# A fused attention and channel-mix kernel: when the loads of batch 1 are issued, and which engine does three small steps of block 0

## The chip, the cores and the metric

The kernel runs on one core of a Trainium2 chip. The metric is the time of one execution on the device in microseconds (us). A profile's span is about 1.8 us shorter than the time of the same execution, so spans are compared with spans and times with times.

## The reference

Cross-covariance attention over four batches of 6208 rows and 256 columns, then a channel mix:

```python
qn = q / (norm(q, axis=1) + 1e-6); kn = k / (norm(k, axis=1) + 1e-6)
a = softmax(kn.transpose(0, 2, 1) @ qn / tau, -1)        # 256 x 256 for each batch
x = v @ a
x_prev = x shifted down by one row, zero first
xk = mu_k * x + (1 - mu_k) * x_prev                      # xr the same with mu_r
k = maximum(xk @ w_k, 0)                                 # 256 -> 1024
out = sigmoid(xr @ w_r) * ((k * k) @ w_v)
```

## The kernel before

The softmax weights of batch 0 need all q and k of batch 0, so the first 36 us read them and sum their products. A serial stretch follows: norms, roots, inverses, scaling, transposes, exp, shares. Then a long loop works on 512-row blocks of x and takes in the products of q and k of batches 1 to 3 between its own. The parts that matter here, with cuts marked by `...`:

```python
v_load(1)                                       # GpSimd queue, in this order
nc.gpsimd.dma_start(w_k_sb, ...)
next_load()                                     # q, k of batch 1, first group
nc.gpsimd.dma_start(w_r_sb, ...)
v_load(2)
nc.gpsimd.dma_start(w_v_sb, ...)
v_load(3)
next_load()
difference, product = x_first()
root(1); root(0)
...
turn_half, take_half = v_first()
invert_first(0)                                 # VectorE, 128x2
evac_first()                                    # VectorE: scale s by 1/|q|
turn_half(0)                                    # TensorE: first half of v of block 0
turn()                                          # TensorE: transpose s
turn_half(1)
keep_warm(2)
go = v_transpose_pe(1, nc.scalar.copy)          # v of block 1
invert_first(1)
take_half(0, nc.vector.tensor_copy)             # first half of v out of PSUM
difference(0)
exp()                                           # ScalarE
go()
weigh_first(0); weigh_first(1)                  # VectorE: shares, a_sb = e * share
take_half(1, nc.vector.tensor_copy)
difference(1)
for a in range(2): ...                          # x and xk of block 0

# in the loop (i = block - 1, j = 0..7)
if i == -1 and j < 3:
    for fh, a in (((0, 0), (1, 0), (0, 1)), ((1, 1),), ())[j]:
        up_first(fh, a)                         # 128 hidden rows, half a block
    if j == 2:
        up(0, 2)
...
if 0 < i + 2 < NBLK and j in (0, 2) and full:
    x_half(i + 2, int(j > 0))                   # 128 columns of x of block i + 2

def up(i, fh): ...
    if fh % 4 == 0 and (i or fh):               # output of the relus: four rows of hidden tiles a buffer
        st[i, "kr", fh // 4] = p2.tile([P, 4, M], BF16, name="kr", tag="kr", bufs=2)
    kr = st[i, "kr", fh // 4][:, fh % 4, :m]
    nc.scalar.activation(kr, kT_ps[:, :m], AF.Relu, scale=0.5 ** 0.5)
```

`square` then reads a `kr` buffer on VectorE (four hidden tiles in one instruction, later two), and frees it. Two such buffers exist.

## Time and profile before

| | before |
|---|---|
| time, median of the first 3 runs | 505.31 us (504.74 to 506.22) |
| span of the profile | 503.1 us |
| TensorE busy | 96% of the span |
| VectorE, ScalarE busy | 85% each |
| serial stretch from the roots to the second x of block 1 | 35.8 to 44.8 us |

How to read it: TensorE is the chain that ended last from 44.8 us on, without a gap. As long as its products stay the same, a kernel of that kind gets shorter only by what moves the start of that unbroken run and opens no gap in it.

### The profile page before, as it was taken

How to read it: one execution, taken by the hardware profiler on the slowest of the kernel's cores; microseconds unless marked ns; L12 is line 12 of the kernel's file. 1: busy time of each engine (PE TensorE's matmuls, PEld its weight loads, DVE VectorE, ACT ScalarE, POOL GpSimd, SP SyncE). 2: the span in 40 equal slices, each digit the busy share in tenths (PEclk: the TensorE clock that was granted, in tenths of full speed). 3: DMA queues.
4: the chain of work that ended last, by engine and by line, in shares of the span. 5: the costliest groups of instructions: out<-in, count | busy, mean ns of one | idle time of the engine just before them, and what ended most of it. 6: DMA issues, size and time to landing. Idle time of an engine off the chain costs nothing.

```text
span 503.1 us, 9303 instructions
## 1 busy us (share of the span) xinstructions
PE 482.3 (96%) x3437; PEld 331.2 (66%) x3437; DVE 429.7 (85%) x787; ACT 428.2 (85%) x871; POOL 96.9 (19%) x143
## 2 busy tenths in 40 slices
PE   2789999999999999999999999999999999999996
PEld 1355677677666766666776666676666666666675
DVE  2788899999988998999889899899888787878784
ACT  4788999899999989888999898988888888788884
POOL 0044322222233132122123323100031010000000
PEclk9999999999999999999999999999999999999999
DMA  8999999999799999997799999982295658344123
GB/s 328 418 314 197 196 185 176 209 210 195 149 187 179 202 166 177 146 203 116 142 191 146 197 171 183 168 150 65 66 207 103 152 86 156 77 105 86 56 71 106
DMA packets 131558, 83.46 MB, mean 166 GB/s; under 512 B 50548, under 2 KB 125624, under 8 KB 130488
## 3 DMA queue, kind: packets, MB, share of 16 engines
q0 software_dynamic: 55840, 33.01, 49.8%
q1 hardware_dynamic: 75352, 49.59, 39.9%
q8 instruction: 27, 0.44, 0.4%
q10 hardware_dynamic: 320, 0.26, 0.2%
q14 instruction: 19, 0.16, 0.1%
HBM read 78.71 MB, written 25.43 MB: 207 GB/s over the span
## 4 chain that ended last, share of the span: by engine, by line
PE 92%; DMA 4%; ACT 2%; DVE 1%; issue 0%; SPq 0%; ACTq 0%; DVEq 0%
PE vr_ps L603 33%; PE kT_ps L571 33%; PE vr_ps L599 8%; PE xT_ps L465 8%; PE s_ps L293 6%; DMA f<-in_k_dram 4%; ACT k L160 1%; PE s_ps L199 1%; ACT qk L155 1%; PE st_ps L353 0%; PE y_ps L643 0%; PE kT_ps L511 0%; PE bank L217 0%; PE vT_ps L425 0%; DVE xk L498 0%
## 5 line engine op out<-in xcount | busy, mean ns | idle before, releaser
L576 ACT ACTIVATE kr<-kT_ps 128x512 bf16<-128x512 f32 (+1 forms) x390 | 234.9, 604 | 33.4 <-PE kT_ps L571 29.7
L603 PE MATMUL vr_ps<-w_v_sb,kk 128*128 128x256 bf16 x1536 | 230.3, 273 | 0.0
L571 PE MATMUL kT_ps<-xk,w_k_sb 128*128 128x512 bf16 (+1 forms) x780 | 229.8, 377 | 0.0
L603 PEld LDWEIGHTS <-kk 128*128 128x128 bf16 x1536 | 150.3, 98 | 57.3
L584 DVE TENSOR_TENSOR kk<-kr 128x2048 bf16<-128x2048 bf16 (+1 forms) x148 | 125.7, 850 | 0.2 <-ACT kr L576 0.2
L613 DVE SCALAR_TENSOR_TENSOR res<-res,vr_ps 128x256 f32<-128x256 f32 x192 | 80.0, 416 | 50.1 <-ACT res L612 50.1
L571 PEld LDWEIGHTS <-w_k_sb 128*128 128x128 bf16 x780 | 75.5, 98 | 27.5 <-issue 0.6
L612 ACT ACTIVATE res<-vr_ps 128x256 f32<-128x256 f32 x192 | 76.7, 399 | 1.3 <-PE vr_ps L603 1.3
L599 PE MATMUL vr_ps<-w_r_sb,xr 128*128 128x256 bf16 x384 | 73.3, 273 | 0.0
L467 ACT CAST xT<-xT_ps 128x512 bf16<-128x512 f32 x94 | 55.9, 595 | 20.0 <-PE xT_ps L465 19.7
L556 DVE SCALAR_TENSOR_TENSOR xr<-delta,mu_t,xT 128x512 bf16<-128x512 bf16 x94 | 70.0, 746 | 0.0
L556 DVE SCALAR_TENSOR_TENSOR xk<-delta,mu_t,xT 128x512 bf16<-128x512 bf16 x94 | 70.0, 745 | 0.0
L599 PEld LDWEIGHTS <-xr 128*128 128x128 bf16 x384 | 37.6, 98 | 44.5 <-issue 0.2
L133 POOL DMA_DIRECT2D qk<-in_q_dram x39 | 26.0, 668 | 169.3 <-ACT kr L576 147.7
L465 PE MATMUL xT_ps<-vT,a_sb 128*128 128x512 bf16 x188 | 55.9, 379 | 0.0
L293 PE MATMUL s_ps<-qk 128*128 128x256 bf16 (+1 forms) x294 | 55.8, 273 | 0.0
L254 ACT ACTIVATE sq<-qk 128x1024 bf16<-128x1024 bf16 x48 | 51.0, 1063 | 0.0
L408 POOL DMA_DIRECT2D v_bf<-in_v_dram x47 | 35.6, 759 | 67.3 <-DMA vT<-v_bf 48.7
L199 PE MATMUL s_ps<-qk 128*128 128x384 bf16 (+2 forms) x98 | 20.2, 357 | 14.8 <-ACT qk L155 14.8
L546 DVE TENSOR_TENSOR delta<-xT 128x1024 bf16<-128x1024 bf16 x47 | 32.2, 686 | 1.1 <-ACT xT L467 1.1
L293 PEld LDWEIGHTS <-qk 128*128 128x128 bf16 (+1 forms) x294 | 28.5, 98 | 5.6 <-issue 0.8
L133 POOL DMA_DIRECT2D qk<-in_k_dram x39 | 25.9, 665 | 3.4 <-DMA w_k_sb<-in_moe_w_k_dram 2.0
(113 smaller groups left out, 252.7 us busy)
## 6 DMA issues: line engine op xcount, KB each, us to landing
out_dram<-res SPq DMA_DIRECT2D x47, 512.0 KB, 4.7
v_bf<-in_v_dram POOLq DMA_DIRECT2D x47, 256.0 KB, 7.3
qk<-in_q_dram POOLq DMA_DIRECT2D x36, 256.0 KB, 6.1
qk<-in_k_dram POOLq DMA_DIRECT2D x36, 256.0 KB, 7.3
f<-in_q_dram SPq DMA_DIRECT2D x4, 1024.0 KB, 13.3
f<-in_k_dram SPq DMA_DIRECT2D x4, 1024.0 KB, 11.0
f<-in_q_dram SPq DMA_DIRECT2D x3, 512.0 KB, 7.6
f<-in_k_dram SPq DMA_DIRECT2D x3, 512.0 KB, 6.2
```

What stands on the lines that cost most here:

```text
L133: nc.gpsimd.dma_start(rows_at(qk, b, g, i)[:rows, :n], qk_src(t, b, g))
L293: nc.tensor.matmul(s_ps[:, ih, :], rows_at(qk, b, g, 0)[:rows, s, ih * P:(ih + 1) * P], rows_at(qk, b, g, 1)[:rows, s, :], start=t0 and ih ...
L465: nc.tensor.matmul(xT_ps, a_sb[:, b, ih, dh * P:(dh + 1) * P], vT[:, :, ih, :], start=ih == 0, stop=ih == 1)
L467: nc.scalar.copy(xT[:, dh, 1:], xT_ps)
L556: nc.vector.scalar_tensor_tensor(o[:, dh], st[i, "d"][:, dh], mu[:, dh:dh + 1], st[i, "x"][:, dh, :M], op0=OP.mult, op1=OP.add)
L571: nc.tensor.matmul(kT_ps[:, :m], w_k_sb[:, dh, fh * P:(fh + 1) * P], xk[:, dh, :m], start=dh == 0, stop=dh == 1)
L576: nc.scalar.activation(kr, kT_ps[:, :m], AF.Relu, scale=0.5 ** 0.5)
L584: nc.vector.tensor_tensor(st[i, "kk"][:, fh // 4 * 4 + lo:fh + 1, :m], kr, kr, op=OP.mult)
L599: nc.tensor.matmul(vr_ps[:, D:], xr[:, dh, s * P:(s + 1) * P], w_r_sb[:, dh, :], start=dh == 0, stop=dh == 1)
L603: nc.tensor.matmul(vr_ps[:, :D], kk[:, fh, s * P:(s + 1) * P], w_v_sb[:, fh, :], start=fh == 0, stop=fh == 7)
L612: nc.scalar.activation(res[:, s], vr_ps[:, D:], AF.Tanh, scale=0.5)
L613: nc.vector.scalar_tensor_tensor(res[:, s], res[:, s], 1.0, vr_ps[:, :D], op0=OP.add, op1=OP.mult)
```

## The change

Its intent: keep GpSimd from writing DMA descriptors while VectorE does the inverses; relieve VectorE of half of v and ScalarE of two relus; fill a hole of TensorE with x of block 1. The diff, cut to its core:

```diff
+    held = const.tile([P, 1], F32, name="held")
 ...
     v_load(1)
     nc.gpsimd.dma_start(w_k_sb, ...)
-    next_load(); w_r_sb; v_load(2); w_v_sb; v_load(3); next_load()
 ...
     go = v_transpose_pe(1, nc.scalar.copy)
+    take_half(0, nc.scalar.copy)
     invert_first(1)
-    take_half(0, nc.vector.tensor_copy)
+    nc.gpsimd.tensor_copy(held, chain_done())     # reads the inverse of the norm of k
+    next_load(); w_r_sb; v_load(2); w_v_sb; v_load(3); next_load()
     difference(0)
 ...
-        nc.scalar.activation(kr, kT_ps[:, :m], AF.Relu, scale=0.5 ** 0.5)
+        if i == 0 and fh in (2, 3):
+            nc.vector.tensor_scalar(kr, kT_ps, 0.0, 0.5 ** 0.5, op0=OP.max, op1=OP.mult)
+        else:
+            nc.scalar.activation(kr, kT_ps[:, :m], AF.Relu, scale=0.5 ** 0.5)
 ...
-                for fh, a in (((0, 0), (1, 0), (0, 1)), ((1, 1),), ())[j]:
+                for fh, a in (((0, 0), (1, 0)), ((1, 1),), ())[j]:
                     up_first(fh, a)
+                if j == 0:
+                    x_half(1, 0)
+                    up_first(0, 1)
 ...
-                if j in (0, 2) and full:
+                if j in (0, 2) and full and (i, j) != (-1, 0):
```

(The loads are shortened to their names.) As in the prediction, part 1 is the hold, part 2 the ScalarE copy, part 3 the earlier x, part 4 the relus on VectorE.

More of the change, by code (lines that the diff above doesn't have):

```diff
@@ L376, in softmax_pieces @@
         if b == 0:
-            return diagonals, root, invert_first, evac_first, turn, exp, weigh_first
+            return lambda: rk[:, 0:1], diagonals, root, invert_first, evac_first, turn, exp, weigh_first
         return [evac, None, norms, roots, pow2, None, invert, None, None, turn, lambda: exp([0]), lambda: exp([1]),
@@ L664, in keep_warm @@
             nc.tensor.matmul(junk_ps, ones, fill, start=True, stop=True)
-    diagonals, root, invert_first, evac_first, turn, exp, weigh_first = softmax_pieces(0)
+    chain_done, diagonals, root, invert_first, evac_first, turn, exp, weigh_first = softmax_pieces(0)
     pending = []
@@ L731 @@
     nc.gpsimd.dma_start(w_k_sb, moe_w_k.rearrange("(ko ki) f -> ki ko f", ki=P))
-    next_load()
-    nc.gpsimd.dma_start(w_r_sb, moe_w_r.rearrange("(ko ki) d -> ki ko d", ki=P))
-    v_load(2)
-    nc.gpsimd.dma_start(w_v_sb, moe_w_v.rearrange("(fo fi) d -> fi fo d", fi=P))
-    v_load(3)
-    next_load()
     difference, product = x_first()
@@ L749 @@
     go = v_transpose_pe(1, nc.scalar.copy)
+    take_half(0, nc.scalar.copy)
     invert_first(1)
-    take_half(0, nc.vector.tensor_copy)
+    nc.gpsimd.tensor_copy(held, chain_done())
+    next_load()
+    nc.gpsimd.dma_start(w_r_sb, moe_w_r.rearrange("(ko ki) d -> ki ko d", ki=P))
+    v_load(2)
+    nc.gpsimd.dma_start(w_v_sb, moe_w_v.rearrange("(fo fi) d -> fi fo d", fi=P))
+    v_load(3)
+    next_load()
     difference(0)
```

## The prediction

> **What bounds the kernel now.** I read the page first, then the chain of waits in order of time, then the timelines of the engines around the hand-over from the first phase (covariance of batch 0) to the long loop, then the time to landing of the transfers. From the page:
>
> ```profile
> PE 482.3 (96%) x3437; PEld 331.2 (66%) x3437; DVE 429.7 (85%) x787; ACT 428.2 (85%) x871; POOL 96.9 (19%) x143
> PE 92%; DMA 4%; ACT 2%; DVE 1%; issue 0%; SPq 0%; ACTq 0%; DVEq 0%
> ```
>
> TensorE is 92% of the chain that ended last. The rest is the first 44 us: input loads, then a serial softmax for batch 0. The chain of waits between 35 and 45 us (start, length, what):
>
> ```profile
> 35.76 0.27 ACT rn L322 x2
> 36.03 0.02 issue
> 36.05 0.48 DVE rn L325
> ...
> 38.20 0.24 PE vT_ps L444 x4
> 38.44 0.03 issue
> 38.47 0.44 DVE vT L447
> 38.93 0.43 DVE delta L479
> 39.35 0.08 DVE sm L373
> ...
> 42.53 0.28 PE kT_ps L511
> 42.84 0.39 ACT kr L513
> 43.23 0.04 issue
> 43.27 0.40 PE kT_ps L511 x2
> 43.67 0.43 PE xT_ps L465 x2
> ```
>
> See three things. A VectorE instruction on 128x2 numbers takes 0.47 us at 36.05. A copy of half of v plus a difference (38.47 to 39.35) stand on VectorE ahead of the reciprocal that the softmax weights wait for. And at 43.23 TensorE, with nothing ahead of it, waits for a relu. From 44.8 us on the chain is TensorE without a gap, so whatever moves that point moves the end; nothing else in this change can. A gain of 2% would be 10.1 us, more than the whole 35.76 to 44.78 stretch (9.0 us), so the sign of a fraction of a microsecond is the real question.
>
> The timeline of the same stretch gives durations (start, length, instruction):
>
> ```profile
> 35.70 0.16 DVE L227 TENSOR_SCALAR less<-mu_t 128x4 f32<-128x4 f32 x1
> 36.05 0.47 DVE L325 TENSOR_SCALAR rn<-rn 128x2 f32<-128x2 f32 x1 [0.19 <-ACT rn L322]
> 37.63 0.34 DVE L325 TENSOR_SCALAR rn<-rn 128x2 f32<-128x2 f32 x1
> 38.47 0.43 DVE L447 COPY vT<-vT_ps 128x512 bf16<-128x512 bf16 x1 [0.30 <-PE vT_ps L444]
> 46.03 0.69 DVE L546 TENSOR_TENSOR delta<-xT 128x1024 bf16<-128x1024 bf16 x1 [1.11 <-ACT xT L467]
> ```
>
> The copy at 38.47 waits for the second group of v transposes, though it reads only what the first group wrote. In the built program its wait is indeed on the last of the second group.
>
> **What the Trainium skill says.** "SBUF — State Buffer", section "Who interferes with whom": VectorE in a two-port mode and GpSimd share a pair of ports under an exclusive lock, and the one that comes second blocks for the whole instruction. The trace agrees in kind: the two L325 took 0.474 and 0.342 us while POOL was writing descriptors, and a like-sized one 0.164 us; casts L157 of 512 columns took 0.61 and 0.67 us under POOL issues, against 0.69 us for 1024 columns. "DMA: Bandwidth & Descriptors", section "Queues, rings and completion order": a DMA engine consumes a ring's descriptors in order. The trace agrees: the GpSimd queue lands in the order of issue. From issue times plus times to landing w_k comes at 34.0 + 7.0 = 41.0 us, w_r at 35.8 + 8.5 = 44.3, w_v at 37.0 + 11.2 = 48.2. "VectorE: DVE Perf Modes", section "Why PSUM operands drop a tier": an fp32 operand in PSUM holds VectorE to its slowest mode. The trace's 128x256 forms from PSUM take 0.416 us (L498, L613).
>
> **The change part by part.**
>
> 1. *Batch 1 loads held.* A one-column GpSimd copy now waits for the second inverse (its wait count is the one that exp has), so POOL writes no descriptors between about 34.7 and 37.7 us. Removed from the path: the excess of the first L325, 0.474 − 0.164 = 0.31 us. Does holding starve the DMA? No: w_k alone keeps the engines busy to 41.0, and the held issues restart near 38, each 0.55 to 0.95 us to issue against 1.25 us or more to move. So I expect the same landings: w_v at 48.2 against a first use at 50.2, v of block 2 at 45.6 (36.5 issue plus its landing) against 47.4. Because the queue is in order, w_k is not faster either. But POOL will now write descriptors from 38 to 43 without the pause that it had (39.3 to 41.3), and that covers the two a_sb scalings (L374, 0.353 us each, SBUF to SBUF). Each may be held up to 0.3 us; as the middle I take 0.15 (one like instruction of 128x256, L341, ranges from 0.336 to 0.494). Cost: 2 × 0.15 = 0.30 us.
>
> 2. *Half of v on ScalarE.* In the built program the ScalarE copy carries the same wait as before, the end of the second v transposes, and it stands ahead of exp on the in-order engine. Exp used to wait only for the transposes of s. With part 1 the second v transposes end at 38.43 − 0.31 = 38.12. A 512-column ScalarE copy takes 0.59 us (as L467) with the next one starting 0.48 to 0.50 later: exp starts at 38.64 (before: 38.27). From exp's start to its accumulator is 0.56 us (38.27 to 38.83 before), so the first reciprocal starts at 39.24 and the first weighing at 39.43, before 39.46. VectorE's relief is thus paid back by the delay of exp: parts 1 and 2 together give 0.03 us by the weights, and with the POOL conflict of part 1 they cost 0.27 us. Everything to the first xk (41.60) hangs behind that.
>
> 3. *x of block 1 earlier.* Before, TensorE had issued the first two up products by 42.86 and then waited to 43.27. The x products of block 1 (2 × 0.22 us of issue) now fill that hole. Later x waits for ScalarE to empty the first half: before 44.73, now about 44.28 as the relu of the third product no longer stands ahead of that copy. TensorE gains 0.43 to 0.45 us at 44.78.
>
> 4. *Two relus on VectorE.* They cost 128x512 from PSUM in fp32: 0.416 us for 256 columns plus 256 more at 1.04 ns makes 0.68 us each, 1.36 us. VectorE idled 1.11 us before delta (46.03), so delta moves to about 46.5 (one relu must also wait for its product), delta 0.69, two xk 1.42: xk of block 1 is done at 48.65 instead of 48.18. TensorE, 0.43 early, wants the second xk at 48.47, so it waits about 0.21. Left of part 3: 0.22 us. The squares end at about 50.95, before the need of 51.1; VectorE's next idle time (1.52 us ahead of the first res, 53.35) takes up the rest. ScalarE loses 2 × 0.57 us, which is no bound here since TensorE has no gap.
>
> Sum: −0.31 + 0.28 (exp behind the copy, net of VectorE's relief) + 0.30 (POOL against the weights) − 0.43 (x earlier) + 0.21 (xk late) = +0.05 us; without the POOL conflict −0.25 us. I lean somewhat to the gain, since the conflict is a matter of chance and ScalarE gets 1.1 us of slack just where it is busiest: −0.2 us, 505.1.
>
> **The rivals.**
>
> - *A clean gain of about 1 us.* For it: if relief of ScalarE lets TensorE run earlier, or the conflict with POOL slowed more than the one L325. Against: no gap of TensorE after 44.8 names ScalarE. It would give 504.3.
> - *A loss by the copy ahead of exp.* If the ScalarE copy with its strided output takes longer than 0.59 us, and both a_sb are blocked the full 0.3 us, parts 1 and 2 cost up to 0.7 us and only 0.2 comes back: 505.8.
> - *Loads late.* If the held loads leave the queue empty, w_v slips. For it: they start 3 us later. Against: the transfers are in order and the queue is full to 41.0. If it slipped by the full 3 us, w_v would land at 51.2, TensorE would lose 1 us and the first units of batch 1 might wait too: about 506.3.
> - *Nothing moves the end.* If the loop's later waits (transposes, POOL's refills) set its pace, 505.3. The chain shows TensorE alone there, so I give it little.
>
> **Range and chances.** The three runs of before span 504.74 to 506.22, 1.5 us, as much as any rival is worth. I put the range at 503.9 to 506.2: from the clean gain less 0.4 of spread, to the late loads without spread. None comes near 10 us, so within 2% is almost certain.
>
> **What would show it.** In the changed kernel's profile: the first L326 (the former L325) near 0.17 us and POOL silent until about 37.7; exp's first start near 38.6 behind the ScalarE copy; the two weighings 0.35 us if free of POOL, 0.5 or more if not, with the second ending near 40.2 or 40.5; x of block 1 directly after the first two up products with no gap of 0.25 us; VectorE relus of 0.68 us; a wait of about 0.2 us for xk near 48.5; w_v landing near 48.2. I am wrong if exp does not move, if w_v lands after 50 us, or if TensorE shows new gaps after 50 us.

## More of the kernel before

All runs but one took 503.8 to 506.6 us; that one took 575.22 us, at a mean granted TensorE clock of 0.854, and is called slow, the others fast. Comparisons of times are of fast runs.

In every trace of this study whose state is fast, the time from the first product for x of block 4 to that of block 20 is 156.8 us, and that from x of block 3 to the end is 444.1 to 444.2 us. Whatever a variant gains or loses is therefore settled within the first 60 us. I use the start of x of block 3 (58.9 us in the kernel before) as the ruler for it.

## The result, and the profile after

The changed kernel took 505.44 us (median of 4, 505.16 to 505.67) against 505.02 (504.70 to 506.22) of the kernel before in the same rounds. The ratio is 1.0004, with a 95% interval of 0.9986 to 1.0022: the same. A repeat of five rounds gave 505.14 against 504.82, ratio 1.0003 (0.9990 to 1.0017).

The page of the changed kernel, engine totals and chain shares:

```profile
PE 481.8 (96%) x3437; PEld 330.9 (66%) x3437; DVE 429.7 (85%) x788; ACT 428.1 (85%) x870; POOL 97.2 (19%) x144
PE 89%; DVE 3%; DMA 3%; ACT 2%; issue 1%; SPq 1%; ACTq 0%; DVEq 0%
```

TensorE's share of the chain fell from 92% to 89% while its busy time stayed, and VectorE rose from 1% to 3%. So something other than TensorE now carries part of the early stretch. The chain of waits of the changed kernel (start, length, what):

```profile
38.13 0.24 PE vT_ps L445 x4
38.37 0.02 issue
38.39 0.59 ACT vT L448
38.98 0.47 ACT e_sb L362 x2
...
44.72 0.69 DVE kr L578
45.41 0.78 DVE xr L499 x2
46.20 0.60 DVE kr L578
46.79 0.61 DVE delta L547
...
47.43 1.42 DVE xk L557 x2
48.84 1.15 DVE kk L588
...
50.09 0.30 ACT kr L580
```

Two things are new. The ScalarE copy of v (38.39) stands in the chain ahead of exp. And from 44.7 to 50.0 us the chain is VectorE, where before it was TensorE: the two relus, xr, delta, xk and the square. Then it goes on over ScalarE and VectorE, and TensorE has it again from 57.8 us. The timeline of the changed kernel (start, length, instruction, idle time before it and what ended that):

```profile
36.28 0.17 DVE L326 TENSOR_SCALAR rn<-rn 128x2 f32<-128x2 f32 x1 [0.20 <-ACT rn L323]
37.98 0.17 POOL L750 COPY held<-rn 128x1 f32<-128x1 f32 x1 [2.89 <-DVE rn L327]
47.55 0.62 PE L426 MATMUL vT_ps<-ident,v_bf 128*128 128x128 bf16 x8 [0.28 <-DMA v_bf<-in_v_dram]
50.09 0.60 ACT L580 ACTIVATE kr<-kT_ps 128x512 bf16<-128x512 f32 x1 [0.37 <-DVE kk L588]
```

The inverse is quick and GpSimd is silent until 37.98, as intended. TensorE waits for v of block 2, which it did not before. ScalarE waits for a square on VectorE, because the relu's output needs the buffer which that square frees.

From 44.52 us (second x of block 1, 0.26 us sooner than before) to x of block 3 at 59.52 us took 15.0 us. Before it was 14.13 us (44.78 to 58.91). So the lead was gained and then more than lost, all between 44 and 60 us. The starts of TensorE's products show where: beyond their usual spacing (0.22 us after a product of 512 columns, 0.11 after 256) they fall behind by 0.44 us at v of block 2 (47.55) and by 0.43 us at 55.9 and 57.8.

### The profile page after: what moved, and what is told of

It is laid out like the page before. It is cut to its first block, busy times and chain, and to the rows that moved or that the text cites. A ratio compares the mean times of both kernels' runs of the same rounds, so it can differ in the third digit from the quotient of the medians.

```text
span 503.7 us, 9299 instructions
## 1 busy us (share of the span) xinstructions
PE 481.8 (96%) x3437; PEld 330.9 (66%) x3437; DVE 429.7 (85%) x788; ACT 428.1 (85%) x870; POOL 97.2 (19%) x144
## 4 chain that ended last, share of the span: by engine, by line
PE 89%; DVE 3%; DMA 3%; ACT 2%; issue 1%; SPq 1%; ACTq 0%; DVEq 0%
PE vr_ps L607 33%; PE kT_ps L572 32%; PE vr_ps L603 8%; PE xT_ps L466 8%; PE s_ps L294 6%; DMA f<-in_k_dram 3%; ACT k L161 1%; PE s_ps L200 1%; SPq L126 1%; DVE kk L588 0%; PE st_ps L354 0%; DVE xk L557 0%; ACT qk L156 0%; PE y_ps L647 0%; DVE k L168 0%
## 5 line engine op out<-in xcount | busy, mean ns | idle before, releaser
L603 PEld LDWEIGHTS <-xr 128*128 128x128 bf16 x384 | 37.6, 98 | 44.7 <-issue 0.4
L466 PE MATMUL xT_ps<-vT,a_sb 128*128 128x512 bf16 x188 | 55.9, 379 | 0.0
```

What stands on the lines that cost most here:

```text
L466: nc.tensor.matmul(xT_ps, a_sb[:, b, ih, dh * P:(dh + 1) * P], vT[:, :, ih, :], start=ih == 0, stop=ih == 1)
L603: nc.tensor.matmul(vr_ps[:, D:], xr[:, dh, s * P:(s + 1) * P], w_r_sb[:, dh, :], start=dh == 0, stop=dh == 1)
```

## The experiments

Twelve runs were made, five rounds each (six for combined), two of them repeats; all were correct. The column "against before" is the mean time of a kernel's fast runs less that of the kernel before in the same rounds. With standard deviations of 0.1 to 0.4 us in five runs (1.0 in the six of combined), such a difference is uncertain by about 0.2 us, and all the 95% intervals of the ratios but one hold 1. The ratios differ from those of these means by up to 0.0003 (hold_x: 1.0002, though its mean is 0.06 us under). The other columns come from the one profile of each run. x of a block is made in two halves of 128 columns; "2nd x" is the start of the second half, and x of block 3 that of its first. Times count from the start of the profile, and the first small scaling starts anywhere from 36.04 to 36.36 us in the fast ones, so a single difference under 0.3 us says little.

| kernel | median us | against before, us | 2nd weighing ends | v of block 2 lands | 2nd x of block 1 | x of block 3 |
|---|---|---|---|---|---|---|
| before, first profile | | | 40.28 | 45.58 | 44.78 | 58.91 |
| before_again | 504.96 | 0.00 | 40.13 | 46.84 | 44.80 | 58.92 |
| after, first profile | 505.44 | | 40.48 | 47.51 | 44.52 | 59.52 |
| after_again | 505.14 | +0.25 | 40.41 | 47.76 | 44.33 | 59.35 |
| hold_only (1) | 505.03 | +0.11 | 40.22 | 46.99 | 44.72 | 58.85 |
| take_only (2) | 505.16 | +0.12 | 40.31 | 46.71 | 44.81 | 58.94 |
| x_early (3) | 504.35 | -0.38 | 40.07 | 46.56 | 43.98 | 58.23 |
| relus_only (4) | 505.31 | +0.67 | 40.04 | 46.54 | 44.54 | 59.36 |
| hold_x (1, 3) | 504.89 | -0.06 | 40.15 | 46.88 | 44.06 | 58.47 |
| relus_back (1, 2, 3) | 504.95 | +0.39 | 40.32 | 47.41 | 44.23 | 59.00 |
| no_hold (2, 3, 4) | 505.44 | +0.54 | 40.34 | 46.56 | 44.25 | 59.26 |
| kr3 (1 to 4, 3rd buffer) | 505.37 | +0.50 | 40.56 | 47.69 | 44.47 | 59.28 |
| relus_kr3 (4, 3rd buffer) | 504.82 | -0.17 | slow | | | |
| combined | 504.64 | -0.18 | 39.81 | 46.63 | 46.43 | 60.55 |

My first theory (A) was that the hold makes w_k late; in the first pair of profiles w_k landed at 41.0 us before and 42.7 after. Its rival (B) was chance.

**before_again.** No edit.

> The unchanged kernel once more, for the spread between profiles. If w_k landing late in the changed kernel (8.3 us after its issue, against 7.0) was chance, this profile may show it too, anywhere from 7 to 8.3 us; if it comes of the hold, this shows 7.0 plus or minus 0.3 us, and w_v landing 11.2 us after issue. Time: ratio 1.000 within 0.001 on both theories.

w_k landed at 42.4 us, 8.1 us after its issue, and the first up product waited for it. The landing at 41.0 us in the first profile was the exception: the ten other fast profiles with w_k in one piece have 42.0 to 42.7. Theory A falls as to w_k. The first small scaling took 0.17 us here, so the 0.47 us that my prediction counted as removable was chance as well.

**after_again.** No edit.

> The changed kernel once more. Theory A (the hold makes the transfers of w_k slower or later): w_k lands 8.0 to 8.6 us after its issue again and the first up product waits for it, 0.4 to 0.7 us. Theory B (chance): near 7.0 us, and the first up product waits for xk alone. Time: A 0.2 to 0.5 us over before, B 0.2 us under it.

w_k at 42.4 us again as in before_again, the time 0.25 us over before. TensorE's largest wait after 44 us is for v of block 2, and it is longer than in the first profile. The timeline of this run, then the same instruction in before_again:

```profile
47.81 0.56 PE L426 MATMUL vT_ps<-ident,v_bf 128*128 128x128 bf16 x7 [0.72 <-DMA v_bf<-in_v_dram]
```

```profile
47.39 0.61 PE L425 MATMUL vT_ps<-ident,v_bf 128*128 128x128 bf16 x8
```

**hold_only.** Part 1 alone:

```diff
+    nc.gpsimd.tensor_copy(held, chain_done())   # after invert_first(1); the six loads follow it
```

> The kernel before with part 1 alone. Both theories: first small scaling 0.17 us instead of 0.47, exp about 0.3 us earlier after its releaser. Theory A: w_k lands 8 us or more after issue, the first up product waits for it about 0.7 to 1.0 us, and the time is 0.4 to 0.9 us longer than before. Theory B: w_k 7.0 us after issue, time 0.2 us shorter.

Nothing is gained and nothing lost (+0.11). w_k landed 7.8 us after its issue and the first up product did not wait for it, so neither theory's forecast held. The first scaling took 0.17 us. v of block 2 lands at 47.0 us, still ahead of its use at 47.3 in this kernel, so the delay is hidden. That the hold does cost the queue shows in the stretches (window, its length, then busy us and count of PE, PEld, DVE, ACT, POOL, granted clock, DMA share, GB/s moved). First before_again, then hold_only:

```profile
40.00:42.00 2.00, 1.76 (x15) 1.16 (x13) 1.44 (x5) 1.38 (x4) 0.05 (x1) 1.00 1.08 171
42.00:44.00 2.00, 1.30 (x9) 0.83 (x10) 2.00 (x6) 1.50 (x5) 0.63 (x2) 1.00 1.16 196
```

```profile
40.00:42.00 2.00, 1.63 (x15) 1.15 (x12) 1.44 (x5) 1.01 (x3) 2.00 (x4) 1.00 0.94 134
42.00:44.00 2.00, 1.62 (x11) 0.91 (x11) 2.00 (x7) 1.66 (x6) 1.39 (x3) 1.00 1.04 177
```

Read the last number and POOL's busy time: with the hold GpSimd is writing descriptors in these windows and the engines move less. From w_k's landing to that of w_r (q, k and w_r between them) it takes 3.13 to 3.31 us in the six fast profiles without the hold and the usual order of loads, and 3.40 to 4.36 us in the six with it. v of block 2 lands at 45.58 to 46.84 us without, at 46.88 to 47.76 with.

**no_hold.** The changed kernel with the loads issued where they were:

```diff
-    nc.gpsimd.tensor_copy(held, chain_done())   # and the six loads back to before x_first()
```

> The changed kernel without part 1: loads issued where they were, the other parts kept. Theory A: w_k lands 7.0 us after issue and nothing waits for it; the first small scaling is at 0.47 us again; exp 0.4 us later than in before; the end 0.1 to 0.3 us sooner than in the changed kernel. Theory B: 0.3 us later than the changed kernel, since the conflict with POOL is back.

v of block 2 lands at 46.56 us and nothing waits for it. Yet the time is no better: +0.54 us. So the late v is not the only thing that loses the lead. The timeline of no_hold: the transposes of v of block 2 without a wait, and ScalarE waiting for the square.

```profile
46.85 0.61 PE L426 MATMUL vT_ps<-ident,v_bf 128*128 128x128 bf16 x8
49.83 0.60 ACT L580 ACTIVATE kr<-kT_ps 128x512 bf16<-128x512 f32 x1 [0.78 <-DVE kk L588]
```

Both theories had put the first scaling at 0.47 us again; it took 0.17. The conflict that the hold is meant to avoid did occur here, but on the second scaling:

```profile
37.40 0.69 DVE L326 TENSOR_SCALAR rn<-rn 128x2 f32<-128x2 f32 x1
```

In the eight profiles without the hold (the slow one included), three of sixteen such instructions took over 0.3 us (0.47, 0.34, 0.69). Each of the three ended within 0.01 us of the end of a DMA issue of GpSimd (at 36.53, 37.97 and 38.09 us), as if held until that was through; but the scaling of before_again at 36.16 us ran inside such an issue (36.10 to 36.84) and took 0.17. In the six with the hold all twelve took 0.16 to 0.17. The hold does what it says. But of those three only one was a first scaling, the one on the path.

The new theory (R): the two relus on VectorE push back the square of the first four hidden tiles, ScalarE needs the buffer that it frees, and from there the full ScalarE queue sets the pace. The rival (E): exp behind the ScalarE copy costs it.

**relus_only.** Part 4 alone on the kernel before:

```diff
+        if i == 0 and fh in (2, 3):
+            nc.vector.tensor_scalar(kr, kT_ps, 0.0, 0.5 ** 0.5, op0=OP.max, op1=OP.mult)
```

> The kernel before with part 4 alone. Theory R: the square of the first four rows begins 0.4 to 0.6 us later than in before (48.1), ScalarE idles for it, x of block 3 at 59.2 to 59.5 us, span 503.4 to 503.6. Theory E: 58.9 or sooner, since exp is not touched and ScalarE is relieved.

+0.67 us, the largest loss in the mean, and the one ratio whose interval leaves out 1 (1.0013, 1.0001 to 1.0026). One run of 506.11 us weighs on it; the other four are 0.52 us over. x of block 3 is at 59.36, as theory R had it, and exp is untouched. The timeline of relus_only has ScalarE waiting for the square; in before_again the same relu follows its neighbour without a gap:

```profile
49.93 0.60 ACT L579 ACTIVATE kr<-kT_ps 128x512 bf16<-128x512 f32 x1 [0.59 <-DVE kk L587]
```

```profile
48.97 1.11 ACT L576 ACTIVATE kr<-kT_ps 128x512 bf16<-128x512 f32 x2
```

The squares begin at 48.59 us in relus_only and at 48.10 in before_again.

**relus_kr3.** Part 4 with a third buffer for the relus' output:

```diff
-    p2.tile([P, 4, M], BF16, name="kr", tag="kr", bufs=2)
+    p2.tile([P, 4, M], BF16, name="kr", tag="kr", bufs=3)
```

> The kernel before with part 4 alone and a third buffer for the relu outputs. If the buffer is the link: no wait of ScalarE for the square, x of block 3 at 58.6 to 59.0 against 59.36 with part 4 and two buffers, span 502.8 to 503.2. If VectorE's lateness acts by another way (xk of block 1, squares for the down products): 59.2 to 59.4.

The four fast runs took 504.78 to 504.92 us, 0.17 less than before, where part 4 with two buffers cost 0.67 in its rounds. One run was slow (575.22 us, clock 0.854), and it is the profiled one, so its times are not compared. The loss of part 4 thus goes with the buffer and not with VectorE's work as such. A third buffer alone, without part 4, was not run; the two profiles of the kernel before show no wait of ScalarE for a square, so there was none for it to remove.

**relus_back.** The changed kernel without part 4.

> The changed kernel with part 4 undone (both relus on ScalarE). Theory R (the VectorE relus push back the square of the first four hidden rows, whose buffer ScalarE needs for its next relu, and from there the ScalarE queue sets the pace): ScalarE does not wait for a square near 50 us, the x of block 3 starts at 58.5 to 59.0 us (59.4 to 59.5 in the changed kernel, 58.9 in the kernel before) and the span is 503.1 or less. Theory E (the delay of exp behind the ScalarE copy is what costs): x of block 3 stays at 59.2 us or later.

ScalarE does not wait for a square, x of block 3 is at 59.00 and the span 503.2, at the edge of what theory R said. But the five runs are 0.39 us over before: undoing part 4 gained nothing that the runs show. In its place TensorE waits for v of block 2 (landed 47.41):

```profile
47.45 0.62 PE L426 MATMUL vT_ps<-ident,v_bf 128*128 128x128 bf16 x8 [0.46 <-DMA v_bf<-in_v_dram]
```

Theory R is right about part 4 and not sufficient for the whole change.

**kr3.** The changed kernel with the third buffer.

> The changed kernel with a third buffer for the relu outputs. Theory R with the buffer as its link: the wait of ScalarE for the square (0.37 us at 50.1 in the changed kernel) is gone and x of block 3 starts 0.2 to 0.5 us sooner than 59.4. If VectorE itself is the bound and not the buffer: 59.4 as before, with TensorE waiting for xk or for the squares instead.

The timeline of ScalarE in kr3:

```profile
48.39 1.01 ACT L434 COPY vT<-vT_ps 128x1024 bf16<-128x1024 bf16 x1 [0.53 <-PE vT_ps L426]
49.30 1.09 ACT L580 ACTIVATE kr<-kT_ps 128x512 bf16<-128x512 f32 x2
```

The wait for the square is gone, and a wait for the transposes of v of block 2 has come ahead of it. x of block 3 is at 59.28, less of a gain than the 0.2 us expected, and the time +0.50 us: no gain. (This profile's first scaling came 0.1 us later than in the two of the changed kernel, so a little may hide there.)

Relus_back, no_hold and kr3 together point to two limits side by side in the changed kernel, the late v of block 2 and the late square. What TensorE's products fall behind their usual spacing from 46 to 60 us (nothing in before_again) bears this out: all at v of block 2 in after_again (0.89 us), relus_back (0.62) and kr3 (0.67); none there in no_hold (0.89) and relus_only (0.70), where it comes at other products from 48.6 us on; and some of each in the first profile of the changed kernel. Each alone eats the lead, so taking away either leaves the other. The changed kernel without both, that is with the third buffer and the old order of loads, was not run, nor parts 2 and 3 without the others; so the share of the ScalarE copy in the late v stays open.

**x_early.** Part 3 alone:

> The kernel before with part 3 alone. Theory R: x of block 1, second half, starts 0.3 to 0.45 us sooner than in before (44.8); of that 0.1 to 0.4 us reaches x of block 3 (58.5 to 58.8), the rest is lost to the full ScalarE queue. Theory E: the same. If ScalarE alone sets the pace already in the kernel before, x of block 3 stays at 58.9 and nothing is gained.

The second x of block 1 starts at 43.98 us, 0.82 sooner than in before_again. Of that 0.27 is the first up product, which began sooner because w_k landed sooner. x of block 3 is 0.69 sooner. The timeline of TensorE in x_early shows x of block 1 right behind the first two up products, without the 0.25 us wait for a relu:

```profile
42.17 0.64 PE L511 MATMUL kT_ps<-xk,w_k_sb 128*128 128x256 bf16 x4 [0.24 <-DMA w_k_sb<-in_moe_w_k_dram]
42.64 0.59 PE L465 MATMUL xT_ps<-vT,a_sb 128*128 128x512 bf16 x2
```

504.35 us against 504.84: the lowest median and 0.38 us on the mean. The interval of the ratio, 0.9980 to 1.0005, still holds 1. Here, too, v of block 2 is at its limit: it landed at 46.56 us and its transposes began at 46.60, so any further lead would first need that load sooner.

**hold_x.** Parts 1 and 3.

> The kernel before with parts 1 and 3, both relus on ScalarE, exp not behind a copy. If the hold makes v of block 2 land late (47.4 to 47.8 us as in the changed kernel, against 46.5) TensorE waits for it 0.4 to 0.7 us and x of block 3 is at 58.7 to 59.0, span 502.9 to 503.2. If the hold is harmless (landing near 46.6): 58.2, span 502.4, as with part 3 alone.

v of block 2 lands at 46.88, TensorE waits 0.11 us for it and loses 0.28 us of issue there, and x of block 3 is at 58.47, 0.24 us later than with part 3 alone. That is less than the stated range. The mean (-0.06) is 0.32 us worse than part 3 alone, about what two such means can differ by. In the four profiles with the hold and the ScalarE copy v of block 2 landed at 47.41 to 47.76, in the two with the hold alone at 46.88 and 46.99. Why the copy should add to it is not settled; the hold ends 0.17 us later with it on the mean. (relus_back is this kernel and the copy, and its mean is 0.45 us worse against before, in other rounds.)

**take_only.** Part 2 alone.

> The kernel before with part 2 alone. Exp starts near 38.7 us instead of 38.05, the second weighing ends near 40.3 instead of 40.1. If the arrival of w_k (42.0 to 42.5 in all runs but one) is what the first up product waits for, that is hidden: x of block 3 at 58.9, span 503.1. If the weights' path counts in full: 59.1, span 503.3.

Exp starts at 38.69 us, 0.64 later than in before_again, and the second weighing ends 0.18 later. The first up product waits for w_k anyway (42.29), so x of block 3 is at 58.94: hidden, as the first branch said.

**combined.** Part 3, the ScalarE copy placed between the two transposes of v so that it waits for the first alone, w_k in two halves, and v of block 2 ahead of w_r:

```diff
     turn_half(0)
+    take_half(0, nc.scalar.copy)
     turn()
```

> Part 3, plus the ScalarE copy of part 2 put ahead of the second v transposes so that it waits for the first alone and stands before exp without delaying it, plus w_k in two halves and v of block 2 ahead of w_r in the queue; no hold, no VectorE relus. Exp near 38.1 us, second weighing ends near 39.6, first up product near 41.5, x of block 3 at 57.7 to 58.1 us, span 501.9 to 502.3; if the full ScalarE queue takes the gain, 58.2 and 502.4 as with part 3 alone.

The weights come 0.3 us sooner (39.81), but the six runs scatter from 503.80 to 506.58 us, and the profile is of the slowest: x of block 3, put at 57.7 to 58.1, came at 60.55. v of block 1 landed at 40.33 us instead of 38.2 to 39.3; that this comes of splitting w_k is not shown, as four things were changed at once. TensorE stood still for 1.26 us, and then each product of 256 columns began 0.21 us after the one before it instead of 0.11. A line of the timeline and two stretches of combined (columns as above):

```profile
40.38 0.93 PE L425 MATMUL vT_ps<-ident,v_bf 128*128 128x128 bf16 x8 [1.26 <-DMA v_bf<-in_v_dram]
```

```profile
39.00:41.00 2.00, 0.74 (x9) 0.63 (x9) 1.54 (x5) 0.23 (x2) 0.57 (x2) 0.88 1.18 174
41.00:44.00 3.00, 3.00 (x17) 2.20 (x16) 0.76 (x2) 1.66 (x3) 1.45 (x3) 0.51 1.13 209
```

The granted clock is 0.51 from 41 to 44 us. The Trainium skill, "TensorE: Matmul & The Clock Gate", section "What's actually happening", has TensorE fall to half its clock after an idle window of some 3.4 us; here the last gap before the fall was 1.26 us. In this trace the clock is 0.5 from 40.53 us on, for 3.41 us (the mean of 0.88 in the first stretch agrees), and in the 3.41 us before that TensorE was busy for 1.80; in the same stretch of the other fast profiles, all at full clock, for 2.46 to 2.74. A longer gap in this trace (1.69 us, from 18.55) left the clock at full, so what set off the fall is not shown. The fastest of the six is the shortest single time, so the order may be worth having if v of block 1 is kept early. That was not tried, and x_early is the version that the runs favour.

## Why the prediction was right or wrong

The forecast of "the same" and the range held: 505.44 and 505.14 us against 505.1. That says little: every rival lay inside 2%, and 505.14 is near the number by luck, since before took 504.82 in those rounds and not 505.3. The lean to a gain did not hold: the means are 0.2 us over before, below what the intervals can tell apart. One of the prediction's own signs of being wrong came true, w_v landing after 50 us (50.15 and 50.40), though nothing waited for it. Another, new gaps of TensorE after 50 us, showed in one of the two profiles. Point by point:

- *What bounds it*: right for what comes after 60 us, which changed in no variant. Wrong in "whatever moves that point moves the end; nothing else in this change can": the second x of block 1 came 0.26 and 0.45 us sooner than in the first profile before, and x of block 3 came 0.61 and 0.44 later, by new waits between 44 and 60 us.
- *Hold, removed excess of 0.31 us*: wrong in size. The first scaling was slow in one of eight profiles without the hold (0.17 or 0.20 us in the seven others), so the mean worth is some 0.04 us. I had taken one event for a rule. The instruction of 0.164 us that I set beside it (35.70 us) also ran while GpSimd was issuing DMAs (35.24 to 36.54), so it was no case without GpSimd.
- *Hold, "the same landings"*: wrong. w_k was indeed not affected, but v of block 2 landed at 46.9 to 47.8 us and w_v at 49.5 to 50.4 instead of 45.6 and 48.2. Part of this was the luck of the first profile. The rest, some 0.1 to 1.2 us for v of block 2, comes with the hold. I argued that issues at 38 us are early enough for a queue full to 41. The runs show the queue moving less between 40 and 44 us. The rival "loads late" was nearer, though the loss is by v of block 2 and not by w_v.
- *GpSimd conflict with the two weighings, 0.30 us*: mostly did not occur. In the six profiles with the hold two of twelve took 0.55 us and ten 0.35, a mean of 0.07 us for the pair. Both were in kernels with the hold but without the ScalarE copy, where the weighings come earlier.
- *Exp behind the ScalarE copy*: right in mechanism. Exp was put at 38.64 and started at 38.87 and 38.80, since the wait on the second transposes of v was kept and the gain ahead of it was not there. By the weights the loss is 0.28 to 0.35 us against before_again; the sum had 0.27, by terms that do not hold singly.
- *x of block 1 earlier, 0.43 to 0.45 us*: right, 0.55 us in x_early after taking off the luck of w_k, and most of the lead reaches x of block 3 there (0.69 of 0.82), though the gain in time is not clear of noise.
- *Relus on VectorE, 0.21 us left on TensorE*: the duration was right (0.68 predicted, 0.69 measured), although L498 took 0.48 us and not the 0.416 that the prediction reads for it; the last xk was done at 48.84 and 48.65 us (48.65 predicted). The step that failed is what the delay costs. I followed xk and the squares to TensorE and took ScalarE to be "no bound", and missed that a relu needs a buffer that a square must free. Part 4 alone cost 0.67 us in the mean and 0.44 us at x of block 3, and TensorE's products fell 0.70 us behind instead of 0.21. With a third buffer on the kernel before the cost is gone.
- *The sum*: terms were added that do not add. The late v and the late square run side by side: with both, TensorE fell 0.87 and 0.89 us behind in the two profiles, no more than with the square alone in no_hold (0.89).

## What to carry to other kernels

Moving work between engines moves the time at which buffers come free; ask for each moved instruction who reuses what it or its followers release, not only whether the engine has time. One profile shows one draw of the chance events (a port conflict, a landing), so an excess seen once is not yet a cost. When two limits lie side by side, undoing one of them shows nothing: test each part alone on the kernel before, not only its absence from the changed one.

## What the Trainium skill lacked or had wrong

- "SBUF — State Buffer", "Who interferes with whom", gives the lock but not how often it bites: of sixteen small VectorE scalings in kernels where GpSimd issues DMAs in that stretch, three took over 0.3 us (0.34, 0.47, 0.69) instead of 0.16.
- "DMA: Bandwidth & Descriptors": no page that I read says that a queue with data still to move slows when its next transfers are issued only 3 to 4 us before it has moved the last ones. Here 640 KB took 3.40 to 4.36 us instead of 3.13 to 3.31. That engines which finish their share of w_k sooner run dry is my guess; no run shows it.
- "TensorE: Matmul & The Clock Gate", "What's actually happening", speaks of an idle window of about 3.4 us and not of how much work such a window may hold: in one profile the clock fell to 0.5 for 3.41 us after a stretch of 3.41 us in which TensorE was busy for 1.80 and had no gap over 1.26, while a gap of 1.69 us earlier in the trace left it at 1.0.
